# 1/rms of each token: VectorE block transpose of repeated columns in place of TensorE transposes, and a new order of work

## The chip, the cores and the metric

The kernel runs on one core of one Trainium2 chip. The metric is device time in microseconds (us), the median of several executions. The core has five engines, each with its own queue of instructions: TensorE (PE, with its weight loads shown as PEld), VectorE (DVE), ScalarE (ACT), GpSimd (POOL) and SyncE (SP), which only issues DMA transfers here.

## The reference

Two layers in a row, all in float32. First a cross read between 512 tokens and 32 state vectors for 8 batches of 8 heads with 64 features:

```python
scores = scale * np.matmul(x, state.transpose(0, 1, 3, 2))   # softmax over the 32 states
xread = np.matmul(a, state)
scores2 = scale * np.matmul(state, x.transpose(0, 1, 3, 2))  # softmax over the 512 tokens
sread = np.matmul(a2, x)
return np.concatenate([xread, sread], axis=2)
```

Then the heads are put side by side, so that each of 8 x (512 + 32) tokens has 512 features, and a gated feed-forward layer with 1536 hidden units follows:

```python
rms = np.sqrt(np.mean(x * x, axis=-1, keepdims=True) + 1e-06)
xn = x / rms * rms_g
g = xn @ w_gate
silu = g * (1.0 / (1.0 + np.exp(-g)))
val = xn @ w_val
return (silu * val @ w_out)
```

The change is about 1/rms of the 512 tokens of a batch.

## The kernel before

**Batches.** A batch's tokens never exist in full: the softmax weights aT_s (256 rows in two tiles of 128 partitions, 512 tokens along the row) are kept, and the state vectors are multiplied into w_gate and w_val for each batch (`own_weights`, L548), which gives small weights v. 1/rms is multiplied into aT_s (L434), so it is needed along the row, the same in all 128 partitions. The 256 state tokens are put through the feed-forward layer at the end (xsT, `state_norm`).

**The hidden layer.** The 1536 hidden units are worked in six pairs (0 to 5), each with gate and value. `hidden_seven` forms the 2x2 block products of a pair with seven products rather than eight. On the PE (L694) their order is: first x and first z of the pair; last x of the pair before; then the second x, the second z, y and the third x of this pair. The letters are PSUM banks: x has two, y and z one each. ScalarE copies x and z out between the products (L740, L743, L745); VectorE adds z and y into the gates g and x into c (three L756), ScalarE takes the tanh (L747), and VectorE gates with L759 and two L771 (the second reads x again); for the later pairs L775 and L781 follow. A pair's first x product needs an x bank that the second L771 of two pairs before has left, and a pair's last x product must come after its third L756, which reads x. `project_seven` does the output layer in the same manner (L856), with ScalarE copies L893 (p1, p5, u2, c21) and VectorE sums L901 and L908.

**The next batch beside it.** While batch b is in its hidden and output layers, batch b+1 has its softmax: `tokens_read` (stream "a"), `states_read` ("s"), its first two products of weights ("w"), and the copies and GpSimd sums of them ("x", L559 and L574 to L577). Steps of `tokens_read` that matter here: the transpose L289, transposes by blocks and a round through DRAM for x (L310, L313, L318), scores L328, softmax L337 to L414, the read L421, squares L428 with sums L431, then `rms_on_blocks`: a transpose by blocks L364, a sum within blocks L367, a matmul with the matrix `groups` (L370), whose result stands in PSUM as 128 partitions x 16 columns: partition 32g+t, column k holds the mean square of token 32k+t, the same in all four groups g of 32 partitions. L375, four times, takes from each group its own four columns, so that 128 partitions x 4 columns hold each token once. GpSimd raises them to the power -1/2 (L271), and the PE transposes each of the four columns, repeated 128 times, into PSUM (L278). L434 reads it there. `slot_sums` on GpSimd (L612 to L615) then forms sums of aT_s for the next batch's products.

**Order of work.** Nothing is scheduled at run time. Within the loop over batches 1 to 7, the string PERIOD gives one letter for each step: the letter's stream (a generator) is run to its next `yield`, and what it emits is queued on the engines in that order. The same string serves all seven turns; in the turn of batch 7, which has no batch after it, the letters "a" run `state_norm` and the first sums of the states' weights, one step at every third "a" (`paced`). Its steps are squares on ScalarE (L510), sums on the PE (L515), their 1e-6 on VectorE and the power on GpSimd (L519, L271), the transposes on the PE (L278), then on VectorE four L525 that scale xsT and four L679. The tiles "at" and "pv" in PSUM have two buffers each, and "xT" and "eS" in SBUF one each; every new use waits for the last reader of the one before.

Of the kernel before, what the change touches and what calls it, by code (L numbers as in the profile page):

```python
# [8 lines left out]
F32 = mybir.dt.float32  # L9
# [3 lines left out]
ALU = mybir.AluOpType  # L13
# [4 lines left out]
P = 128  # L18
# [10 lines left out]
)  # L29

PERIOD = (
    "hhvthttxhauhhxhuauaahhtutaahtahvxvtuhuxxhuuhthtxuthuhtuhhuhuhhutuhutthuxuhxtxuhh"
    "vhuuthhxthxtahuhathuuuxuuauthuthtahhuthuuuhuhpuuuhtuuucauapaaasaspkacpaspsspaaaa"
    "aaaapkkcpccaakaaascuskaappkaaaaapssssaaaaksapkakasswwwxxpxkxxpccssx"
)

STATES = (
# [6 lines left out]
def kernel(  # L44
# [21 lines left out]
    VE, SE, GE, TE = nc.vector, nc.scalar, nc.gpsimd, nc.tensor  # L66

    B, H, S, D = x.shape
    Ns = state.shape[2]
    DM = H * D  # L70
    DFF = moe_w_gate.shape[1]
    NC = S // P
# [7 lines left out]
    consts = ctx.enter_context(tc.tile_pool(name="consts", bufs=1))  # L80
    one = ctx.enter_context(tc.tile_pool(name="one", bufs=1))
    two = ctx.enter_context(tc.tile_pool(name="two", bufs=2))
# [26 lines left out]
    def load_x(b, *queues):  # L109
# [8 lines left out]
        for c in range(NC):  # L118
# [3 lines left out]

    ident = consts.tile([P, P], F32, name="ident")
    make_identity(nc, ident)
    mhalf = consts.tile([P, NC], F32, name="mhalf")
    GE.memset(mhalf, -0.5)
    ones = consts.tile([P, 1], F32, name="ones")
    GE.memset(ones, 1.0)

    GE.tensor_tensor(out=consts.tile([P, NC], F32, name="first_pow"), in1=mhalf,  # L130
                     in0=ones.to_broadcast([P, NC]), op=ALU.pow)
    bounds = consts.tile([P, 2], F32, name="bounds")
    GE.memset(bounds[:, 0:1], 1151.0 + 7.5 / 16)
# [4 lines left out]
    for i in range(4):  # L138
        GE.tensor_copy(groups[:, i], ident[:, 0:Ns])
        for j in range(1, 4):  # L140
            GE.tensor_tensor(out=groups[:, i], in0=groups[:, i],
                             in1=ident[:, Ns * j:Ns * j + Ns], op=ALU.add)
# [125 lines left out]
    def mean_root(ss, n):  # L268

        ri = two.tile([P, NC], F32, name="ri")  # L270
        GE.tensor_tensor(out=ri[:, 0:n], in0=ss, in1=mhalf[:, 0:n], op=ALU.pow)  # L271
        return ri

    def along_rows(ri, n):

        rp = aps.tile([P, NC, P], F32, name="at")
        for c in range(n):
            TE.transpose(out=rp[:, c, :], in_=ri[:, c:c + 1].to_broadcast([P, P]), identity=ident)  # L278
        return rp.rearrange("p c t -> p (c t)")
# [80 lines left out]
    def rms_on_blocks(b, sq):  # L360


        n = S // Ns
        VE.transpose(out=sq[:, 1, :], in_=sq[:, 0, :])  # L364
        yield
        part = one.tile([P, n], F32, name="part")
        VE.reduce_sum(out=part, in_=sq[:, 1, :].rearrange("p (k f) -> p k f", f=Ns), axis=AXX)  # L367
        yield
        sp = aps.tile([P, n], F32, name="at")
        TE.matmul(out=sp, lhsT=groups.rearrange("p i t -> p (i t)"), rhs=part,  # L370
                  start=True, stop=True)
        yield
        ss = two.tile([P, NC], F32, name="ss")
        for g in range(4):
            VE.tensor_scalar(ss[Ns * g:Ns * g + Ns], sp[Ns * g:Ns * g + Ns, g::4], 1e-6, None,  # L375
                             op0=ALU.add)
        yield "step"
        ri = mean_root(ss, NC)
        yield
        rp = along_rows(ri, NC)  # L380
        yield
        return rp

    def tokens_read(b):
# [45 lines left out]
        for i, j in ((0, 1), (2, 3), (0, 2)):  # L430
            VE.tensor_tensor(out=sq[:, i, :], in0=sq[:, i, :], in1=sq[:, j, :], op=ALU.add)  # L431
            yield
        rp = yield from (rms_on_array if b < 2 else rms_on_blocks)(b, sq)
        VE.tensor_tensor(out=aT_s[b], in0=aT_s[b],  # L434
                         in1=rp.unsqueeze(1).to_broadcast([P, 2, S]), op=ALU.mult)
# [71 lines left out]
    def state_norm():  # L507

        sq = one.tile([P, NI, NT], F32, name="sqT", tag="eS")
        SE.activation(out=sq, in_=xsT, func=ACTF.Square, scale=DM ** -0.5)  # L510
        yield
        sp = aps.tile([P, NT // P], F32, name="at")
        for r in range(NT // P):
            for i in range(NI):
                TE.matmul(out=sp[:, r:r + 1], lhsT=sq[:, i, P * r:P * r + P], rhs=ones,  # L515
                          start=(i == 0), stop=(i == NI - 1))
        yield
        ss = two.tile([P, NT // P], F32, name="sst")
        VE.tensor_scalar(ss, sp, 1e-6, None, op0=ALU.add)  # L519
        ri = mean_root(ss, NT // P)  # L520
        yield
        rp = along_rows(ri, NT // P)
        yield
        for i in range(NI):
            VE.scalar_tensor_tensor(out=xsT[:, i, :], in0=xsT[:, i, :], scalar=rms_g[:, i:i + 1],  # L525
                                    in1=rp[:, 0:NT], op0=ALU.mult, op1=ALU.mult)
        sums_of_x()
        yield
# [143 lines left out]
    def sums_of_x():  # L672

        tt = seven["late"].tile([P, 3, HI, P], F32, name="x_t")
        b11, b12, b21, b22 = blocks_of_x()
        x_sums.extend(tt[:, i] for i in range(3))
        for to, a, b in ((tt[:, 0], b12, b11), (tt[:, 1], b22, tt[:, 0]), (tt[:, 2], b21, tt[:, 1]),
                         (b12, b22, b12)):
            VE.tensor_tensor(out=to, in0=a, in1=b, op=ALU.subtract)  # L679
# [319 lines left out]
    for b in range(1, B):  # L999
        if b + 2 < B:  # L1000
            load_state(b + 2)
            load_x(b + 2)
        h, t, u = hidden_seven(S, weights_of(b), lambda b=b: tokens_of(b), False)
        p, c, k = project_seven(S, store_tokens(b))
        own = [own_weights(b, mp) for mp in range(2, NM // 2)]
        then = [own_weights(b + 1, mp) for mp in range(2)] if b + 1 < B else []
        others = None
        streams = {"h": h, "t": t, "u": u, "p": p, "c": c, "k": k,
                   "v": (step for part in own for step in part[0]),
                   "x": (step for part in own + then for step in part[1])}  # L1010
        if b + 1 < B:
            streams.update(a=tokens_read(b + 1), s=states_read(b + 1),
                           w=first_products(b + 1, then))
        else:
            others = paced(step for part in (state_norm(), sums_of_w([0])) for step in part)
            streams["a"] = others
        with tc.manual_schedule(**by_hand):
            for stream in PERIOD:
                if stream in streams:
                    step = next(streams[stream], done)  # L1020
                    assert step is not done or b + 1 == B
        assert all(next(stream, done) is done for stream in streams.values() if stream is not others)
    n = B * (NM // 2)
# [37 lines left out]
```

## Time and profile before

| | |
|---|---|
| time, median of 3 | 779.46 us (779.45 to 780.23) |
| span of the profiled execution | 777.7 us |
| PE busy | 765.8 us, 98% |
| DVE busy | 536.7 us, 69% |
| ACT busy | 325.6 us, 42% |
| POOL busy | 161.6 us, 21% |
| L278, transposes of 1/rms (PE) | 34, 274 ns each from start to end |
| L271, power on 128x4 (POOL) | 8, 1158 ns each |
| L375, 32x4 (DVE) | 24, 158 ns each |

The share of an engine is its busy time over the span. Matmuls overlap in the pipeline, so a mean of 274 ns is the time through it; what a matmul costs in a full stream is the distance from its start to the next one's. A line's number is that of the kernel before throughout.

### The profile page before, as it was taken

Reading aid. Unit: us, or ns where it says so; the run is one execution under the profiler, and the core shown is the slowest. Engines: PE = TensorE matmul, PEld = TensorE weight load, DVE = VectorE, ACT = ScalarE, POOL = GpSimd, SP = SyncE. Lnnn points to the kernel's source line nnn. Section 1 sums busy time; section 2 is a strip of 40 time slices with the busy share of each in tenths; the row PEclk is TensorE's granted clock in tenths of the full one; section 3 lists DMA queues with packets and bytes.
Section 4 is the critical chain, followed back from the end, with each engine's and each line's share of the span. In section 5 each row is a group of like instructions: output and inputs, shape, how many; then the busy total and the mean of one; then the engine's idle time right before and its main releaser. Section 6 shows DMA issues by size and latency. Waiting matters only on the chain.

```text
span 777.7 us, 12111 instructions
## 1 busy us (share of the span) xinstructions
PE 765.8 (98%) x4722; PEld 586.2 (75%) x4722; DVE 536.7 (69%) x846; ACT 325.6 (42%) x536; POOL 161.6 (21%) x232
## 2 busy tenths in 40 slices
PE   6999999999999999999999999999999999999998
PEld 4643344688877887878878877888778878888996
DVE  4999996678647882888468864787378735881461
ACT  4998874553135322542255314532344314510320
POOL 2100003430053104320433015400631043300000
PEclk9999999999999999999999999999999999999999
DMA  9789764670266225630466026612543154100311
GB/s 290 200 293 322 274 175 173 184 255 14 85 190 247 79 72 177 238 115 20 160 207 214 1 95 219 248 39 68 204 163 109 41 176 163 55 14 27 123 55 28
DMA packets 73689, 113.00 MB, mean 145 GB/s; under 512 B 40864, under 2 KB 51616, under 8 KB 66720
## 3 DMA queue, kind: packets, MB, share of 16 engines
q1 hardware_dynamic: 60512, 92.75, 35.1%
q10 hardware_dynamic: 13120, 19.47, 8.5%
q8 instruction: 38, 0.62, 0.3%
q14 instruction: 19, 0.16, 0.1%
HBM read 87.56 MB, written 24.64 MB: 144 GB/s over the span
## 4 chain that ended last, share of the span: by engine, by line
PE 92%; DVE 5%; DMA 1%; SPq 1%; issue 0%; ACT 0%; DVEq 0%
PE f L694 38%; PE f L856 35%; PE f L796 5%; PE pv L590 4%; PE at L548 3%; PE pv L548 3%; PE at L328 1%; DVE ex L249 1%; PE at L490 1%; PE at L421 1%; DVE raw L245 1%; DMA raw<-in_moe_w_gate_dram 1%; DVE w_m L254 1%; DVE top L242 1%; DMA rows<-in_state_dram 0%
## 5 line engine op out<-in xcount | busy, mean ns | idle before, releaser
L856 PE MATMUL f<-wo,hb 128*128 128x256 f32 x540 | 123.0, 382 | 0.0
L694 PE MATMUL f<-aT_s,v 128*128 128x256 f32 x504 | 119.7, 382 | 0.0
L856 PEld LDWEIGHTS f<-wo,hb 128*128 128x128 f32 x540 | 101.5, 190 | 23.1 <-issue 5.0
L694 PEld LDWEIGHTS f<-aT_s,v 128*128 128x128 f32 x504 | 93.6, 190 | 24.3 <-DVE c L756 5.9
L756 DVE TENSOR_TENSOR g<-g,f 128x512 f32<-128x512 f32 (+1 forms) x96 | 61.4, 651 | 68.6 <-PE f L694 40.3
L694 PE MATMUL f<-aT_t,vs 128*128 128x256 f32 x336 | 87.1, 382 | 0.0
L747 ACT ACTIVATE hb<-g 128x1024 f32<-128x1024 f32 (+1 forms) x48 | 48.2, 1004 | 87.6 <-DVE g L756 87.6
L856 PE MATMUL f<-wt,hs 128*128 128x256 f32 x360 | 80.4, 379 | 0.0
L271 POOL TENSOR_TENSOR ri<-ss,mhalf 128x4 f32<-128x4 f32 x8 | 9.3, 1158 | 340.9 <-DVE ss L375 233.5
L893 ACT COPY ot<-f 128x256 f32<-128x256 f32 x60 | 20.1, 371 | 134.7 <-PE f L856 126.0
L856 PEld LDWEIGHTS f<-wt,hs 128*128 128x128 f32 x360 | 68.3, 190 | 9.4 <-issue 0.2
L694 PEld LDWEIGHTS f<-aT_t,vs 128*128 128x128 f32 x336 | 63.2, 190 | 14.9 <-issue 5.9
L759 DVE SCALAR_TENSOR_TENSOR hb<-hb,g 128x1024 f32<-128x1024 f32 x42 | 53.8, 1282 | 13.1 <-ACT hb L747 13.1
L574 POOL TENSOR_TENSOR vs<-v 128x256 f32<-128x256 f32 x42 | 30.5, 726 | 144.2 <-ACT v L559 144.2
L559 ACT COPY v<-pv 128x512 f32<-128x512 f32 x42 | 22.9, 595 | 67.7 <-PE pv L548 67.7
L745 ACT COPY g<-f 128x512 f32<-128x512 f32 (+1 forms) x48 | 26.9, 559 | 56.3 <-PE f L694 56.3
L796 PE MATMUL f<-wo,hb 128*128 128x512 f32 x96 | 44.7, 600 | 0.0
L590 PE MATMUL pv<-aT_s,v 128*128 128x512 f32 x96 | 43.7, 595 | 0.2 <-DVE aT_s L434 0.2
L694 PE MATMUL f<-aT_s,vs 128*128 128x256 f32 x168 | 43.1, 379 | 0.0
L694 PE MATMUL f<-aT_t,v 128*128 128x256 f32 x168 | 43.1, 379 | 0.0
L856 PE MATMUL f<-wo,hs 128*128 128x256 f32 x180 | 41.5, 382 | 0.0
L856 PE MATMUL f<-wt,hb 128*128 128x256 f32 x180 | 40.8, 383 | 0.0
(142 smaller groups left out, 1241.1 us busy)
## 6 DMA issues: line engine op xcount, KB each, us to landing
w_m<-w_d SPq DMA_DIRECT2D x48, 1024.0 KB, 5.7
out_dram<-ot SPq DMA_DIRECT2D x56, 128.0 KB, 1.8
raw<-in_moe_w_val_dram SPq DMA_DIRECT2D x6, 1024.0 KB, 5.5
raw<-in_moe_w_out_dram SPq DMA_DIRECT2D x6, 1024.0 KB, 7.8
x_b<-in_x_dram SPq DMA_DIRECT2D x96, 64.0 KB, 2.4
w_d<-w_m SPq DMA_DIRECT2D x6, 1024.0 KB, 4.9
x_d<-xB ACTq DMA_DIRECT2D x6, 1024.0 KB, 4.3
xG<-x_d ACTq DMA_DIRECT2D x24, 256.0 KB, 5.0
```

Of the source, the lines that this page charges most:

```text
L548: TE.matmul(out=pv[e][Ns * j:Ns * j + Ns, :], lhsT=stT_g[b][D * e:D * e + D, j, :], rhs=w[D * e:D * e + D, j].rearrange("p m k f -> p (m k ...
L559: SE.copy(v[:, e].rearrange("p m k f -> p (m k f)"), pv[e])
L574: GE.tensor_tensor(out=vs[:, 0], in0=a21, in1=a22, op=ALU.add)
L590: TE.matmul(out=to[0], lhsT=lhs(i, k), rhs=r, start=(i == 0), stop=(i == len(rhs) - 1))
L694: TE.matmul(out=ps[:, i, 0:half], lhsT=l[:, i, :], rhs=r, start=(start and i == 0 and k == 0), stop=(k == len(lhs) - 1), skip_group_check= ...
L745: SE.copy(gates(q)[1], q["x"][:, :, 0:half])
L747: SE.activation(out=hb[:, 2 * mp:2 * mp + 2, 0:n].rearrange("p m (c t) -> p m c t", c=2), in_=q["g"][:, :, :, 0:half], func=ACTF.Silu if s ...
L756: VE.tensor_tensor(out=to, in0=to, in1=q[ps][:, :, 0:half], op=ALU.add)
L759: VE.scalar_tensor_tensor(out=h, in0=h, scalar=1.0, op0=ALU.add, op1=ALU.mult, in1=q["g"].rearrange("p m c t -> p m (c t)"))
L796: TE.matmul(out=banks[r], lhsT=hb[:, m, P * r:P * r + P], rhs=wo[:, m, :], start=(m == 0), stop=(m == NM - 1))
L856: TE.matmul(out=banks[name][:, r, :], lhsT=lhs(k)[:, P * r:P * r + P], rhs=rhs(k), start=(start and r == 0 and k == 0), stop=(k == HM - 1) ...
L893: SE.copy(to, banks[name][:, r, :])
```

## The change

In batches 2 to 7 each group of 32 partitions keeps all 16 columns, so it holds 1/rms of all 512 tokens. A VectorE transpose works on blocks of 32x32, within a group of 32 partitions: given column k repeated 32 times, it puts token 32k+t at place t of block k in every one of the 32 partitions. So one instruction lays 1/rms along the row in all 128 partitions, and the four PE transposes and their PSUM tile are not needed; the result goes into a free part of sq in SBUF. Batches 0 and 1 (`rms_on_array`) and the states keep the PE's way. PERIOD is dealt anew for this, with as many steps of each stream as before, and `state_norm` loses two of its `yield`s.

```diff
-    mhalf = consts.tile([P, NC], F32, name="mhalf")
+    mhalf = consts.tile([P, S // Ns], F32, name="mhalf")
...
 def rms_on_blocks(b, sq):
...
-        ss = two.tile([P, NC], F32, name="ss")
-        for g in range(4):
-            VE.tensor_scalar(ss[Ns * g:Ns * g + Ns], sp[Ns * g:Ns * g + Ns, g::4], 1e-6, None,
-                             op0=ALU.add)
+        ss = two.tile([P, n], F32, name="ssb")
+        VE.tensor_scalar(ss, sp, 1e-6, None, op0=ALU.add)
         yield "step"
-        ri = mean_root(ss, NC)
-        yield
-        rp = along_rows(ri, NC)
+        ri = two.tile([P, n], F32, name="rib")
+        GE.tensor_tensor(out=ri, in0=ss, in1=mhalf, op=ALU.pow)
+        yield
+        rp = sq[:, 2, :]
+        VE.transpose(out=rp, in_=ri.unsqueeze(2).to_broadcast([P, n, Ns]))
         yield
         return rp
...
 def state_norm():
...
                 TE.matmul(out=sp[:, r:r + 1], lhsT=sq[:, i, P * r:P * r + P], rhs=ones,
                           start=(i == 0), stop=(i == NI - 1))
-        yield
         ss = two.tile([P, NT // P], F32, name="sst")
         VE.tensor_scalar(ss, sp, 1e-6, None, op0=ALU.add)
         ri = mean_root(ss, NT // P)
         yield
         rp = along_rows(ri, NT // P)
-        yield
         for i in range(NI):
             VE.scalar_tensor_tensor(out=xsT[:, i, :], in0=xsT[:, i, :], scalar=rms_g[:, i:i + 1],
                                     in1=rp[:, 0:NT], op0=ALU.mult, op1=ALU.mult)
```

The new PERIOD moves, on the PE, the scores L328 from the output layer into the last pairs of the hidden layer, the read L421 from behind the second wt,hs group of L856 to ahead of it, the first two L548 of the next batch to straight behind L370, L490 into the middle of the last L856 group, and the L548 of pairs 3 and 4 forward within pair 0 of the hidden layer. On VectorE the blocks' transposes and the softmax move with them. PERIOD itself:

```diff
-    "hhvthttxhauhhxhuauaahhtutaahtahvxvtuhuxxhuuhthtxuthuhtuhhuhuhhutuhutthuxuhxtxuhh"
-    "vhuuthhxthxtahuhathuuuxuuauthuthtahhuthuuuhuhpuuuhtuuucauapaaasaspkacpaspsspaaaa"
-    "aaaapkkcpccaakaaascuskaappkaaaaapssssaaaaksapkakasswwwxxpxkxxpccssx"
+    "hhvthtaxhxthauhvuvthhtauhthxhaahtuuxxuxahuhuatthtuuhxhhuutuxhuhthhuhuttauhxthhhu"
+    "ahuuuavhattuhtxuhhxhutuuauuthaaauhaxhhthtutuhuhuhuuuaptuuuhupuacpaaaaaaaapaaaapa"
+    "kacaakapssaaaaaspcsspakcakkcaaucksaawwsxwxppxksssxppskkpsxskpcxsscs"
```

More of the change, by code (lines that the diff above doesn't have):

```diff
@@ L128 @@
     GE.memset(ones, 1.0)
-    GE.tensor_tensor(out=consts.tile([P, NC], F32, name="first_pow"), in1=mhalf,
+    GE.tensor_tensor(out=consts.tile([P, NC], F32, name="first_pow"), in1=mhalf[:, 0:NC],
                      in0=ones.to_broadcast([P, NC]), op=ALU.pow)
```

## The prediction

> **What bounds the kernel now.** I read the page's busy shares first, then the list of waits of the PE, the PE's timeline over one whole batch, and last the timelines of the batch where the state norm runs.
>
> The busy shares and the chain of work that ended last:
>
> ```profile
> PE 765.8 (98%) x4722; PEld 586.2 (75%) x4722; DVE 536.7 (69%) x846; ACT 325.6 (42%) x536; POOL 161.6 (21%) x232
> PE 92%; DVE 5%; DMA 1%; SPq 1%; issue 0%; ACT 0%; DVEq 0%
> ```
>
> The PE is never free and the chain runs through it. A busy PE is not proof by itself, so the list of what PE matmuls waited for comes next:
>
> ```profile
> PE at L289 <- DMA rows<-in_state_dram: 5.9, 1, 5.9
> PE at L548 <- DVE w_m L254: 0.9, 1, 0.9
> PE at L328 <- ACT xT L302: 0.7, 1, 0.7
> PE at L348 <- DVE sq L431: 0.6, 1, 0.6
> PE pv L590 <- DVE aT_s L434: 0.2, 1, 0.2
> ```
>
> All of these lie in the opening stage. In batches 1 to 7 the PE waits for nothing, so in them time is won only by taking work off the PE, and lost by any wait that reaches it. The PE's timeline round the edited steps of one period:
>
> ```profile
> 374.47 2.75 PE L856 MATMUL f<-wo,hs 128*128 128x256 f32 x12
> 377.06 0.29 PE L370 MATMUL at<-part,groups 128*128 128x16 f32 x2
> 377.20 2.84 PE L856 MATMUL f<-wo,hs 128*128 128x256 f32 x12
> 379.88 0.60 PE L278 MATMUL at<-ident,ri 128*128 128x128 f32 x4
> 380.41 1.10 PE L490 MATMUL at<-x_b,e2T 128*32 128x64 f32 x64
> 381.44 1.09 PE L548 MATMUL pv<-w_m,stT_g 64*32 64x512 f32 x16
> ```
>
> Columns are start, length, what. Read starts against starts: the four transposes hold the PE from 379.88 to 380.41, 0.53 us. One period is 83.47 us (the score matmuls of L328 start at 181.92 and at 265.39 in the chain).
>
> [...] L364 and L310 transpose 128x512 in blocks in 0.69 to 0.71 us. [...] VectorE sits 4.45 us before L756 in each period, held by a wait that the view puts on L289. [...]
>
> **The change part by part.**
>
> *Batches 2 to 7, PE.* Four transposes go, six times. The slot is 0.53 us; ahead of it 0.09 us is lost (the L856 group begun at 377.20 has 12 passes of 0.2158, 2.59, and the next thing starts 2.68 later). So at most 0.62 a period. But the new order on the PE sets L490 alone between two L856 groups. Where it stands alone in the opening stage it holds the PE 1.12 us instead of 1.03 and leaves 0.08 on either side: 0.25 us given back. Between 0.27 and 0.62, I take 0.4: 6 x 0.4 = 2.4 us saved (1.6 to 3.7). All other PE work is the same instructions in another order.
>
> *Batches 2 to 7, VectorE and GpSimd.* Four L375 of 0.16 us become one of about 0.2; a transpose of 128x512 (0.7 by L364) is added. The power goes from 4 columns (1.16 us by L271) to 16. Two columns took 0.70, so 0.23 a column and an estimate of 3.9 us; the other bound is 1.2. Behind it on VectorE wait the transpose, L434 and the L901 of p5; behind it on GpSimd the slot sums. In the new order L370 comes 18.9 us ahead of the next batch's first product (two L548 groups, 60 passes of L856, L490, L502), where it was 11.6. With sum 0.5, power 3.9, transpose 0.7, L434 1.2 and four slot sums of 0.73 the chain needs about 9.5 us: hidden, at either bound. The L901 on p5 has to be done before the wt,hb products; that is 12.3 us after L370, and it needs about 8.
>
> *The other moves in a period.* Score matmuls move ahead of the last products of pair 4; from them to L421 the PE now has 20.8 us of work, and VectorE needs it for two pairs of gates and the softmax. Counting its starts in the trace (0.60 a 512-column pass, 1.2 for L759, 2.65 from L407 to L414), the second aT_s half is done about 1.5 us ahead of L421. The L548 pair at mp 0 and 1, moved up behind L370, needs a PSUM buffer that L374 frees: 0.6 us ahead. For xG the last load is issued about 7.7 us ahead and lands in 5.0 (6.3 at most). I cost these at nothing; the hiding work is the PE's own queue.
>
> *Batch 7, state norm.* This is the part I charge. Two yields went, so the sum L519 and the power are issued in one step with the matmuls L515, and L525 and the four L679 in one step with L278. Before, they were steps apart:
>
> ```profile
> 646.40 1.84 PE L515 MATMUL at<-ones,sqT 128*128 128x1 f32 x16
> 648.28 0.16 DVE L519 TENSOR_SCALAR sst<-at 128x2 f32<-128x2 f32 x1
> 674.78 0.38 PE L278 MATMUL at<-ident,ri 128*128 128x128 f32 x2
> 685.91 1.65 DVE L525 SCALAR_TENSOR_TENSOR xsT<-xsT,rms_g,at 128x256 f32<-128x256 f32 x4
> 687.48 0.42 DVE L679 TENSOR_TENSOR x_t<-xsT 128x256 f32<-128x256 f32 x1
> ```
>
> L519 met a result just ready, and L525 ran 10.7 us after L278, in the projection, where nothing on the PE stood behind it. In the changed kernel's order VectorE has L519 straight behind the third add (L756, c) of pair 0, and ahead of pair 0's L759 and L771. The PE has L515 only after the second z product of pair 1. Take 0 as the start of batch 7's first product (639.14 before), 0.864 us a product:
> - The PE comes to L515 at 12.8. Its PSUM tile is one of the two of the L548 pair; ScalarE empties that behind pair 1's L745, at about 13.2. L515 runs 13.3 to 15.0: 0.5 us of wait.
> - VectorE, idle since 7.3, does L519 at 15.2, L759, L771, L771 until 17.8 (1.26 + 0.61 + 0.68). The last frees the x bank that pair 2's first product needs. The PE is there at 16.7 and starts at about 18.1: 1.3 us.
> - L278 follows at 19.0 to 19.2, L525 and L679 from 19.5 (3.16 us by the starts 685.91 and 689.07), and only then the L756 add of pair 1, done at 23.4. Pair 1's last product must not write x before it; it would have run at 20.1: 3.4 us.
>
> Queued behind these waits on VectorE are pair 0's and pair 1's gates, and the PE waits for both. Sum 5.2 us, in one batch, once. After it VectorE is again ahead of the PE, and the work moved forward (L651 and L653 into pairs 3 to 5) leaves c of pairs 4 and 5 0.6 to 0.8 us to spare. The projection gets nothing in return, since the PE had no wait there.
>
> *Sum.* 779.46 - 2.4 + 5.2 = 782.3 us.
>
> **The rivals.**
> 1. The wait in batch 7 is absorbed and only the PE's saving remains: 779.46 - 2.4 = 777.1, faster. For it: six batches have the clean gain. Against: the x bank and the add of pair 1 are true dependences, and VectorE is in order. 0.16.
> 2. Half of the wait shows, because the L515 result comes earlier than I place it or VectorE does L525 and L679 quicker: 2.4 us against 2.4, 779.5, the same. Against: 1.57 and 1.59 us for these eight are measured. 0.08.
> 3. On top of the forecast a wait appears in each period, at L421 or at L328 where I have 1.5 us to spare: some 0.7 x 6 = 4, so 786.3. For it: softmax and gates now share VectorE. Against: margins by the trace's own durations. 0.10.
> 4. The forecast, 0.66.
>
> **How the numbers follow.** With saving 1.6 to 3.7 and wait 4.3 to 6.0 (without the L515 part, or with 0.3 more on each wait), the forecast covers 780.1 to 783.9. Rival 1 reaches down to 777.0 with the estimate of 2.4 us. The upper end, 785.5, leaves most of rival 3 outside. Range 777.0 to 785.5. Of the forecast's 0.66 about 0.04 lies within 0.2% (below 781.0), so slower 0.62 + 0.10 = 0.72, same 0.04 + 0.08 = 0.12, faster 0.16.
>
> **What would show it.** Right: no L278 in batches 2 to 7, the L328 to L328 period at about 83.1, no PE wait in it; in batch 7 the PE waits on VectorE's L771 and on the c add of L756, the stretch from batch 7's first product to its first L856 grows from 41.9 us to about 47, and VectorE shows a long wait for L515. Wrong: batch 7's stretch unchanged, or a period above 83.5 (then L421, L328 or L374 is where I look), or a power far above 5 us.

## The result, and the profile after

The changed kernel takes 789.47 us (median of four, 788.03 to 791.89) against 779.46 us before: a ratio of 1.0132, 95% interval 1.0104 to 1.016, some 10 us slower. The profiled execution is at the lower end, 788.03 us, with a span of 786.2 us against 777.7: 8.5 us to account for in the traces. From L517 of the kernel before on, the changed kernel's numbers are one or two lower (L519 is now L518, L525 is L523, L548 is L546, L694 is L692, L756 is L754, L771 is L769, L856 is L854); the lines above keep theirs, but the new transpose is L380.

The busy shares and the chain that ended last, of the changed kernel:

```profile
PE 764.7 (97%) x4698; PEld 583.2 (74%) x4698; DVE 540.6 (69%) x834; ACT 325.0 (41%) x536; POOL 179.6 (23%) x232
PE 82%; DMA 8%; DVE 8%; issue 1%; ACTq 1%; ACT 0%; SPq 0%
```

The 24 transposes are gone (4722 to 4698 PE instructions) and 1.1 us of PE busy time with them, but the chain no longer runs through the PE alone: DMA has gone from 1% of it to 8%, VectorE from 5% to 8%. What the PE waited for (us in total, times, longest), the five lines of the list that are new:

```profile
PE at L490 <- DMA e2T<-e_d: 5.2, 5, 2.0
PE f L692 <- DVE c L754: 3.1, 1, 3.1
PE f L692 <- DVE hb L769: 1.0, 1, 1.0
PE at L515 <- ACT v L557: 0.3, 1, 0.3
PE at L490 <- issue: 0.2, 1, 0.2
```

The waits for c, hb and v are the state norm in batch 7. The two at L490, 5.4 us in six times, are in the periods. The PE's timeline in the first of them (start, length, what, and in brackets the idle time before and what ended it):

```profile
201.96 0.29 PE L370 MATMUL at<-part,groups 128*128 128x16 f32 x2
202.18 1.09 PE L546 MATMUL pv<-w_m,stT_g 64*32 64x512 f32 x16
203.06 1.06 PE L546 MATMUL at<-w_m,stT_g 64*32 64x512 f32 x16
...
218.41 1.10 PE L490 MATMUL at<-x_b,e2T 128*32 128x64 f32 x64 [1.13 <-DMA e2T<-e_d]
```

L490 needs the exponents of the states' read, which go from eB to DRAM (e_d, L475) and come back transposed (e2T, L479). The chain of waits in the same stretch:

```profile
203.95 1.17 DVE eB L472
...
205.14 8.78 DMA e_d<-eB
...
215.34 2.98 DMA e2T<-e_d
```

The write takes 8.78 us. Over the six batches, from the view of line L475, in the changed kernel:

```profile
DMA to landing us min/median/max: 7.6/7.8/9.1
```

Before, the same view of the same line:

```profile
DMA to landing us min/median/max: 2.6/2.6/3.6
```

What lies in front of the write is seen in the timeline of the two issuing queues (SPq is SyncE's, ACTq ScalarE's):

```profile
203.40 1.19 SPq L169 DMA_DIRECT2D w_m<-w_d  x2
...
205.14 0.35 ACTq L475 DMA_DIRECT2D e_d<-eB  x1
```

The two L546 at 202.18 and 203.06 are the last readers of two weight buffers, so as they finish, SyncE fetches the next two weights, 1024 KB each. In the kernel before these L548 stood behind L490, which had started at 380.41, and the loads went out after it:

```profile
368.31 0.35 ACTq L475 DMA_DIRECT2D e_d<-eB  x1
...
382.90 1.53 SPq L169 DMA_DIRECT2D w_m<-w_d  x2
```

The write itself does not go out later than before: it is issued 12.1 us ahead of L490 there (368.31 and 380.41), and 12.1 us ahead of the time at which the PE comes to L490 here (205.14 and 217.28).

The periods, from the first L328 of a batch to that of the next, are 84.34, 85.21, 83.40, 84.10 and 83.93 us, where each was 83.47 to 83.48. The idle times before L490 in them are 1.13, 2.01, 0.19, 0.89 and 0.72, and 0.44 in batch 7's preparation: 5.4 us together. Each period is 83.2 and its idle time.

In batch 7, the timelines of the PE and VectorE:

```profile
655.79 1.95 PE L515 MATMUL at<-ones,sqT 128*128 128x1 f32 x16 [0.30 <-ACT v L557]
657.77 0.16 DVE L518 TENSOR_SCALAR sst<-at 128x2 f32<-128x2 f32 x1 [7.95 <-PE at L515]
660.53 1.10 PE L692 MATMUL f<-aT_s,v 128*128 128x256 f32 x4 [0.97 <-DVE hb L769]
661.89 1.66 DVE L523 SCALAR_TENSOR_TENSOR xsT<-xsT,rms_g,at 128x256 f32<-128x256 f32 x4 [0.31 <-PE at L278]
665.05 0.68 DVE L754 TENSOR_TENSOR c<-c,f 128x512 f32<-128x512 f32 x1
665.79 1.13 PE L692 MATMUL f<-aT_t,v 128*128 128x256 f32 x4 [3.07 <-DVE c L754]
```

VectorE stands 7.95 us at L518 with the gates of pair 0 behind it, and the PE waits for them (hb). Behind L278, L523 and four L677 stand ahead of pair 1's last addition (c), and the PE waits again. The hidden layer from the first product (642.53) to the first L854 (689.63) is 47.1 us, where it was 41.9 (the three brackets of the PE are 4.3 of these 5.2; a wait can hide in the modelled ends of the matmuls ahead of it); from there to the end nothing comes back (96.6 us in both).

So the 8.5 us of the two traces are 5.2 in batch 7, 5.4 before L490, and about 2.0 won back. Of these 2.0 some 0.4 us lie in the opening (batch 1's first product at 134.78, before at 135.16), whose length varies by as much from trace to trace. The rest of the 10 us between the medians is in executions other than the profiled one.

### The profile page after: what moved, and what is told of

Its sections match the earlier page's. It is cut to its first block, busy times and chain, and to the rows that moved or that the text cites. A ratio compares the mean times of both kernels' runs of the same rounds, so it can differ in the third digit from the quotient of the medians.

```text
span 786.2 us, 12078 instructions
## 1 busy us (share of the span) xinstructions
PE 764.7 (97%) x4698; PEld 583.2 (74%) x4698; DVE 540.6 (69%) x834; ACT 325.0 (41%) x536; POOL 179.6 (23%) x232
## 4 chain that ended last, share of the span: by engine, by line
PE 82%; DMA 8%; DVE 8%; issue 1%; ACTq 1%; ACT 0%; SPq 0%
PE f L692 37%; PE f L854 27%; DMA e_d<-eB 5%; PE f L794 5%; PE pv L588 4%; PE at L546 3%; DMA e2T<-e_d 2%; PE pv L546 2%; PE at L328 1%; DVE ex L249 1%; PE at L490 1%; PE at L421 1%; DVE raw L245 1%; ACTq L479 1%; DVE eB L472 1%
## 5 line engine op out<-in xcount | busy, mean ns | idle before, releaser
L854 PE MATMUL f<-wo,hb 128*128 128x256 f32 x540 | 123.9, 382 | 0.0
L692 PE MATMUL f<-aT_s,v 128*128 128x256 f32 x504 | 120.7, 382 | 1.0 <-DVE hb L769 1.0
L854 PEld LDWEIGHTS f<-wo,hb 128*128 128x128 f32 x540 | 101.5, 190 | 23.1 <-issue 9.9
L692 PEld LDWEIGHTS f<-aT_s,v 128*128 128x128 f32 x504 | 94.0, 190 | 24.7 <-issue 12.4
L692 PE MATMUL f<-aT_t,vs 128*128 128x256 f32 x336 | 87.8, 384 | 0.0
L754 DVE TENSOR_TENSOR g<-g,f 128x512 f32<-128x512 f32 (+1 forms) x96 | 61.3, 651 | 33.9 <-PE f L692 26.1
L854 PE MATMUL f<-wt,hs 128*128 128x256 f32 x360 | 80.4, 379 | 0.0
L692 PEld LDWEIGHTS f<-aT_t,vs 128*128 128x128 f32 x336 | 62.6, 190 | 20.4 <-issue 11.7
L572 POOL TENSOR_TENSOR vs<-v 128x256 f32<-128x256 f32 x42 | 32.8, 780 | 188.2 <-ACT v L557 188.2
L854 PEld LDWEIGHTS f<-wt,hs 128*128 128x128 f32 x360 | 68.3, 190 | 9.4 <-issue 0.2
L377 POOL TENSOR_TENSOR rib<-ssb,mhalf 128x16 f32<-128x16 f32 x6 | 19.7, 3289 | 177.2 <-DVE ssb L374 177.2
L899 DVE TENSOR_TENSOR ot<-ot,f 128x256 f32<-128x256 f32 x45 | 17.4, 414 | 58.7 <-PE f L854 54.3
L557 ACT COPY v<-at 128x512 f32<-128x512 f32 x54 | 29.1, 593 | 56.0 <-POOL vs L575 31.1
L692 PE MATMUL f<-aT_t,v 128*128 128x256 f32 x168 | 43.3, 380 | 3.1 <-DVE c L754 3.1
L692 PE MATMUL f<-aT_s,vs 128*128 128x256 f32 x168 | 43.1, 379 | 0.0
L854 PE MATMUL f<-wt,hb 128*128 128x256 f32 x180 | 41.8, 383 | 0.0
```

What stands on the lines that cost most here:

```text
L557: SE.copy(v[:, e].rearrange("p m k f -> p (m k f)"), pv[e])
L572: GE.tensor_tensor(out=vs[:, 0], in0=a21, in1=a22, op=ALU.add)
L692: TE.matmul(out=ps[:, i, 0:half], lhsT=l[:, i, :], rhs=r, start=(start and i == 0 and k == 0), stop=(k == len(lhs) - 1), skip_group_check= ...
L754: VE.tensor_tensor(out=to, in0=to, in1=q[ps][:, :, 0:half], op=ALU.add)
L854: TE.matmul(out=banks[name][:, r, :], lhsT=lhs(k)[:, P * r:P * r + P], rhs=rhs(k), start=(start and r == 0 and k == 0), stop=(k == HM - 1) ...
```

## The experiments

The theory after the first reading, T: the loss is the order's, in two parts that have nothing to do with each other, the wait of the state norm in batch 7 and the write of e_d behind two weight loads; the 1/rms code itself saves. Rival 1: the longer chain of 1/rms (the power on GpSimd, the transpose on VectorE) holds the periods up. Rival 2: the PE's new order costs time on the PE itself.

**rms_alone.** The new 1/rms code in the kernel before; PERIOD and the two yields stay.

```diff
...
-        ri = mean_root(ss, NC)
-        yield
-        rp = along_rows(ri, NC)
+        ri = two.tile([P, n], F32, name="rib")
+        GE.tensor_tensor(out=ri, in0=ss, in1=mhalf, op=ALU.pow)
+        yield
+        rp = sq[:, 2, :]
+        VE.transpose(out=rp, in_=ri.unsqueeze(2).to_broadcast([P, n, Ns]))
```

> The new 1/rms code (one add, pow of 128x16, one block transpose) in the order of the kernel before, with both yields of the state norm kept. Theory (the loss comes from the order: state norm in batch 7, and the e_d write queued with the w_m loads): no L490 wait, e_d lands in under 4 us, stretch of batch 7 near 41.8 us, and what is left is the clean saving of a period without L278: between 0.07 us (the one waitless period of after, 83.40 against 83.47) and the 0.4 us of the prediction, times 6: 777.0 to 779.1 us. Rival 1 (the longer pow and the longer chain on VectorE hold up each period): first products of batches 2 to 7 come later, periods of 83.8 or more, 781 us or more.

Measured: 785.27 us, ratio 1.0069 (1.0055 to 1.0082). The expectation of T missed; the time is that of rival 1. The write lands in 2.6 us and there is no L490 wait, but every period is 84.45 to 84.46. VectorE and the PE in one of them (L380 is the new transpose, L498 the read of L490's PSUM tile, L548 the next user of that tile):

```profile
382.52 0.71 DVE L380 STREAM_TRANSPOSE sq<-rib 128x512 f32<-128x512 f32 x1 [2.11 <-POOL rib L377]
...
384.59 0.47 DVE L498 TENSOR_SCALAR sr<-at,z 128x64 f32<-128x64 f32 x2
385.20 1.09 PE L548 MATMUL at<-w_m,stT_g 64*32 64x512 f32 x14 [0.37 <-DVE sr L498]
```

L498 could have run when L490 had ended, at about 382.9. In VectorE's order it stands behind L380 and L434, and L380 waits for the power. Through L498 that reaches the PE: from L490 to the L856 behind the L548 pair it is 4.33 us, where it was 2.90 (the bracket has 0.37 of the 1.43; the rest is counted as busy time of the two L548 matmuls ahead, whose ends are modelled). So the chain does cost time in the old order, though not as its own length, and the next run asks whether this is all.

**sr_first.** rms_alone with a few letters of PERIOD moved, so that L498 comes ahead of L380.

```diff
-    "aaaapkkcpccaakaaascuskaappkaaaaapssssaaaaksapkakasswwwxxpxkxxpccssx"
+    "aaaapkkcpccaakaaascuskaappkaaaaapssssaaaaksapkkssaawwwxxpxkxxpccssx"
```

> The kernel rms_alone (new 1/rms code in the order of before) with three letters of PERIOD moved, so that VectorE does L498 (the read of the PSUM tile that L548 waits for) ahead of the transpose L380, which waits for the pow. Theory (what rms_alone lost, 1.0 us a period, is L498 held up in VectorE's own order behind the pow of 2.9 to 3.3 us, and the saving of L278 itself is real): L548 no longer waits, periods of 83.05 to 83.2 us against 83.47, that is 2.0 to 2.5 us under before: 776.5 to 777.5 us. Rival (the pow or the block transpose slows the period in another way): periods stay at 84.4, 785 us.

Measured: 776.79 us, ratio 0.9961 (0.9948 to 0.9973), under the kernel before. Every period is 83.04. The same place (the power takes 2.91 us in both runs):

```profile
379.24 0.48 DVE L498 TENSOR_SCALAR sr<-at,z 128x64 f32<-128x64 f32 x2 [0.64 <-PE at L490]
379.63 0.70 DVE L380 STREAM_TRANSPOSE sq<-rib 128x512 f32<-128x512 f32 x1
379.99 1.06 PE L548 MATMUL at<-w_m,stT_g 64*32 64x512 f32 x16
```

L380 no longer waits, since the power has ended by the time L498 is done, and L548 no longer waits either. No wait of the PE is left in the periods, and this is the saving in the old order: 0.43 us a period, 2.6 in six.

**order_alone.** The changed kernel with the old `rms_on_blocks`: the diff of the 1/rms code undone, PERIOD and the yields as changed.

```diff
-        ss = two.tile([P, n], F32, name="ssb")
-        VE.tensor_scalar(ss, sp, 1e-6, None, op0=ALU.add)
+        ss = two.tile([P, NC], F32, name="ss")
+        for g in range(4):
+            VE.tensor_scalar(ss[Ns * g:Ns * g + Ns], sp[Ns * g:Ns * g + Ns, g::4], 1e-6, None,
+                             op0=ALU.add)
...
-        GE.tensor_tensor(out=ri, in0=ss, in1=mhalf, op=ALU.pow)
-        yield
-        rp = sq[:, 2, :]
-        VE.transpose(out=rp, in_=ri.unsqueeze(2).to_broadcast([P, n, Ns]))
+        ri = mean_root(ss, NC)
+        yield
+        rp = along_rows(ri, NC)
```

> The new order and the yields taken out, with the old 1/rms code (four adds, pow of 128x4, along_rows with its matmuls L278). Theory: the whole loss of after stays, and L278 comes back on top, 0.1 to 0.4 us a period: 790 to 792 us, e_d landing in 7 us or more, L490 wait of about 1 us a period, stretch of batch 7 near 47. Rival 1 (the new 1/rms code costs the time in the periods): periods fall back to about 83.5 and only batch 7's 5.2 us stay: 784 to 786 us.

Measured: 811.41 us, ratio 1.0405 (1.039 to 1.0421); both forecasts missed by 19 us or more. In its list of PE waits:

```profile
PE at L278 <- POOL ri L271: 14.2, 6, 2.4
```

In the new order L278 comes on the PE straight behind L370, before add and power can be done. 2.4 us of a period of 87.1 to 88.2 is this wait. The PE's timeline behind it:

```profile
204.83 0.65 PE L278 MATMUL at<-ident,ri 128*128 128x128 f32 x4 [2.43 <-POOL ri L271]
205.41 1.09 PE L546 MATMUL pv<-w_m,stT_g 64*32 64x512 f32 x16
206.29 2.02 PE L546 MATMUL at<-w_m,stT_g 64*32 64x512 f32 x16
```

The second L546 takes 2.02 us where it takes 1.06 in the changed kernel: fourteen of its matmuls start only when L434 on VectorE, which reads L278's result in PSUM, has ended (it runs from 205.95 to 207.17). These 0.96 us, the wait of 2.43 and 0.58 for L278 itself make 87.2 of 83.2. Two of the five periods are that long (87.11 and 87.18); in the other three slower passes come on top (in the third the second L546 takes 2.84 us, and the L854 group behind it 5.69 where 5.45 is usual), and the mean granted clock of the execution is 0.987. The write of e_d lands in 3.0 us (2.6 to 4.1) here: the L546 pair is held up behind L278, and the weight loads with it (206.62 in the same period, behind the write at 205.95). As a test of T the run says little. It shows that the order needs the new code; rms_alone shows that the code needs another order than the old one.

**fetch_behind.** The changed kernel with one thing moved: the two weight loads that the early L546 release go out on ScalarE's queue behind the fourth e2T load.

```diff
-    def fetch(n):
+    held = []
+
+    def fetch(n, queue=nc.sync):
         if NM // 2 <= n < (B + 1) * (NM // 2):
-            nc.sync.dma_start(out=new_w(n), in_=w_d[n % (NM // 2)])
+            queue.dma_start(out=new_w(n), in_=w_d[n % (NM // 2)])
...
                                     in_=e_d[b % 2][:, :, g].rearrange("j t f -> t j f"))
+                while g == 3 and held:
+                    fetch(held.pop(0), nc.scalar)
                 yield
...
-            fetch(b * (NM // 2) + mp + W_BUFS)
+            if b > 1 and mp < 2:
+                held.append(b * (NM // 2) + mp + W_BUFS)
+            else:
+                fetch(b * (NM // 2) + mp + W_BUFS)
```

> After, with the two w_m loads of mp 0 and 1 held back and issued on ScalarE's queue behind the fourth e2T load, instead of right behind the L546 that free their buffers. Theory: the e_d write lands in 2.6 to 4 us again, PE no longer waits at L490, the periods come to 83.1 to 83.5 us, and 3.5 to 5.2 us go: 784.3 to 786.0 us, with batch 7's norm wait (stretch of 47) unchanged. Rival 1 (pow and VectorE chain) and rival 2 (a slower order of matmuls on PE itself): periods stay at 84 us, 788.5 to 790 us.

Measured: 783.14 us, ratio to before 1.005 (1.0033 to 1.0067), 6.3 us under the changed kernel's 789.47 and 1.2 under the range that T gave. The write and L490 (L476 and L493 here):

```profile
DMA to landing us min/median/max: 2.6/2.6/4.3
```

```profile
383.94 1.10 PE L493 MATMUL at<-x_b,e2T 128*32 128x64 f32 x64
```

No wait, and all five periods are 83.14. Rival 1 and rival 2 fall for the new order: with the same chain of 1/rms and the same order on the PE the periods are 0.33 shorter than before.

**one_behind.** As fetch_behind, but only one of the two loads is put behind.

```diff
-            if b > 1 and mp < 2:
+            if b > 1 and mp == 1:
```

> As fetch_behind, but only one of the two w_m loads (mp 1) is put behind the e2T loads; the one of mp 0, 1024 KB, stays in front of the e_d write. Theory (time to landing grows with the bytes queued ahead, and PE waits only once it passes about 7.4 us, the shortest landings of after having given waits of 0.2 us): e_d lands in 4 to 6 us, no wait at L490, 782.5 to 784 us, as with both behind. Rival (each load costs its share of the loss): half of it stays, about 785.5 to 786.5 us.

Measured: 783.78 us, ratio 1.0053 (1.0038 to 1.0069). The write (L476):

```profile
DMA to landing us min/median/max: 4.6/5.4/6.6
```

Nothing ahead, one load, two loads: 2.6, 5.4, 7.8 us at the median. The time is fetch_behind's. The PE waits at L493 once, 0.4 us, and there it was not the write (5.2 us) that was long, but a load of e2T behind it, with 5.58 us where 3 are usual. The longest write, 6.6 us, made nothing wait, and in the changed kernel one of 7.8 us cost 0.19: the order leaves the write 4 to 5 us of room, and the loss begins where that is used up.

**pow_twice.** fetch_behind with each power done twice.

```diff
-        GE.tensor_tensor(out=ri, in0=ss, in1=mhalf, op=ALU.pow)
+        for _ in range(2):
+            GE.tensor_tensor(out=ri, in0=ss, in1=mhalf, op=ALU.pow)
```

> fetch_behind with the pow of each period done twice on GpSimd, 3.3 us more ahead of the transpose in six periods. Theory (in the new order pow and transpose have about 10 us to spare before the first matmul that takes the slot sums): no change, 782.7 to 783.8 us. Rival (the chain of 1/rms is on the path in the new order as in rms_alone): 1 to 3 us more per period, 789 us or more.

Measured: 783.09 us, ratio 1.005 (1.0033 to 1.0066), periods 83.14, though GpSimd's pair takes 6.27 us. In fetch_behind's order the power is hidden with room to spare.

**norm_late.** The changed kernel with the state norm of batch 7 begun later.

```diff
+LATE = 18
...
-    def paced(steps):
+    def paced(steps, late):
+        yield from range(late)
         while True:
...
-            others = paced(step for part in (state_norm(), sums_of_w([0])) for step in part)
+            others = paced((step for part in (state_norm(), sums_of_w([0])) for step in part), LATE)
```

> After, with 18 of the letters a of batch 7 let go by before the state norm starts, so that its matmuls L515 and L278 and its VectorE work come about where the kernel before had them (behind the last pairs of the hidden layer). Theory: the stretch of batch 7's hidden layer falls from 47.1 to 41.8-42.3 us, the waits of L692 on c and hb go, 5.2 us less: 783.8 to 785.0 us, periods and L490 waits unchanged. Rival: the norm was hidden in after too, or its wait is only moved to the states' first products: 788 us or more.

Measured: 785.82 us, ratio 1.0087 (1.0056 to 1.0117), six executions from 781.23 to 789.92; the median is 0.8 us above the range that was expected. The waits on c and hb are gone. From batch 7's first product to the end of the profiled span it is 139.6 us (143.7 in the changed kernel, 138.6 before): 4.1 of the 5.2 are won. L515 and L278 came too late this time, both in the projection, and the PE waits for the power there:

```profile
699.91 0.43 PE L279 MATMUL at<-ident,ri 128*128 128x128 f32 x2 [1.04 <-POOL ri L272]
```

The L490 waits are all still there, 7.4 us in the profiled execution, which is the slowest of the six; that the spread comes from them is not shown, since the other five have no trace.

**both.** fetch_behind, with the two yields back and the norm's steps set by hand at letters a of batch 7, so that L515 comes 15.4 us and L278 35.7 us after the first product, and the VectorE work behind the last pair.

```diff
+        yield
         ss = two.tile([P, NT // P], F32, name="sst")
...
         rp = along_rows(ri, NT // P)
+        yield
         for i in range(NI):
...
-            if next(steps, done) is done:
-                break
-            yield from range(3)
+        for k in itertools.count():
+            if k in (0, 6, 9, 13, 17) or k > 17 and k % 4 == 0:
+                if next(steps, done) is done:
+                    break
+            yield
```

> After with both causes taken out: the two w_m loads of mp 0 and 1 issued behind the e2T loads, and the state norm of batch 7 with its two yields back and its five steps at the letters a number 0, 6, 9, 13 and 17, so that L515 comes behind pair 2, the pow behind pair 4's sums, L278 in pair 6 and the VectorE work behind the last pair. Theory: the losses add (5.2 us in batch 7, 4.9 us at L490), periods of 83.14, stretch of batch 7 near 41.8: 783.1 - 5.2 = 777.9 us, range 777.3 to 778.5, 1 to 2 us under before. Rival (the two waits partly hide each other): 780 us or more.

Measured: 777.40 us, ratio 0.9972 (0.9962 to 0.9982), faster than before. The PE waits for nothing from batch 7's first product to its projection, and from that product to the end it is 138.6 us, as before. The two losses add: 6.3 us from the loads, 5.7 from the norm, and what remains against before is the saving of six periods. The profiled execution, 779.26 us, is the slowest of the eight, and the others are at most 777.72. In it one period is 84.66 instead of 83.14: there the four loads of xG landed in 7.9 to 9.3 us (4.9 at the median in the changed kernel), and the PE waited for them at the scores, L330 here. In the other traces no such wait shows.

## Why the prediction was wrong

The forecast was 782.3 us, in a range from 777.0 to 785.5; measured were 789.47. The direction held, and so did the charge it rested on. One term, put at nothing, was 5.4 us in the profile.

- *What bounds the kernel*: right. Whatever was followed up here moved the time by PE work removed, by a wait that reached the PE, or, in norm_late, by slower passes behind such a wait (granted clock 0.66 over five us).
- *The saving, 2.4 us*: the mechanism holds and the size is a little high for this order. It is 0.33 us a period, 2.0 in six, by fetch_behind, and 0.43 a period by sr_first, in the old order. The difference of 0.10 is all that the new order costs on the PE, L490 standing alone included, and 0.25 had been set aside for that; the slot itself gave less than the 0.62 it was taken from.
- *Batch 7, state norm, 5.2 us*: right in sum and in its places. VectorE kept the order it was given, as the forecast took it to: it stood 7.95 us at L518, with the gates of pair 0 behind it. L515 began 13.26 us after the first product (13.3 said), L518 at 15.24 (15.2), the x product of pair 2 at 18.0 (18.1), the last x product of pair 1 at 23.26 (23.4). The waits themselves show as 0.30, 0.97 and 3.07 us against 0.5, 1.3 and 3.4. The stretch is 47.1 us, and both takes 5.7 off by undoing it.
- *The power*: 3.29 us against an estimate of 3.9, hidden, as said; pow_twice shows it would be at double the length. The estimate started from 1.16 us for 128x4, a mean over eight that the opening's power of 1.99 us raises; in the periods it took 1.02. From there and the 0.70 of two columns it is 0.16 a column and 2.9 us, which is what rms_alone shows.
- *The other moves in a period*, costed at nothing: this step failed. L421, L328 and L374 were looked at, and none of them waits in the changed kernel. Of the moved L548 pair the prediction asked what it needs, a PSUM buffer, and not what it gives free. Its end releases two weight loads of 1024 KB, and 15 us ahead of L490 they go in front of the 512 KB write that L490 depends on. The prediction names neither the loads nor the write, so the write's landing of 2.6 us, true of the old order, stood for the new one too; it was 7.8. The missing term is 5.4 us in the profile, and 6.3 between the medians of after and fetch_behind. With it the sum is 779.46 - 2.0 + 5.2 + 5.4 = 788.1, where the profiled execution was 788.03; that it comes so close is partly luck, since the median is 1.4 us above that and 0.4 of the 2.0 lay in the opening.
- *The rivals*: the third, a further wait in each period at 786.3 us, had the right form, a wait in each period, and the wrong place. The first two, less loss in batch 7, did not occur. The range's upper end, 785.5, took in batch 7's wait and little of a second one.

The prediction did not ask why the L548 pair had been moved. rms_alone and sr_first show what the old order does with the new code: a read of a PSUM tile that the PE wants back stands behind VectorE's wait for the power. Moving the pair is one way out of that, and it brought the wait for the write; moving L498 is another, and no wait of the PE came of it.

What stays open: how much of the changed kernel's 1.5 us between its profiled execution and the difference of the medians is the clock, below, and why xG landed late in one execution of the run both.

## What to carry to other kernels

When work is moved forward, list what its end releases, not only what it waits for: here two buffers that came free started two loads, and a write that had landed in 2.6 us without them landed in 7.8 behind them. A landing time read in the old order is a property of that order; before a transfer is costed at it again, look up what will be in flight beside it, and how much room its reader has. (The 1024 KB write of x_d, too, lands in 7.9 us at the median in the changed kernel, 4.3 before; no wait came of it.) And an instruction that waits on a slower engine should be dealt behind any read that gives a PSUM tile back to the PE: with L380 ahead of L498 the periods were 84.45 us, behind it 83.04.

## What the runs showed of the hardware

A write on one queue landed later with large loads issued ahead of it on another: 512 KB on ScalarE's queue landed in 2.6, 5.4 and 7.8 us at the median with none, one and two loads of 1024 KB issued ahead of it on SyncE's (fetch_behind, one_behind and the changed kernel). Each load ahead added 2.4 to 2.8 us, about as much as the whole write takes alone.

The power's time on GpSimd grew with the columns in these runs, and was not the same in every order of work. Beside the same VectorE instructions it took 1.02 us for 128x4 (before) and 2.92 for 128x16 (rms_alone), about 0.16 a column; in the new order 1.52 for 128x4 (order_alone) and 3.29 for 128x16. Batch 7's power of 128x2 took 0.70 us before and 1.62 in the changed kernel. What makes these differ was not tested. The VectorE block transpose of 128x512 took 0.71 us at L364, and at L380 too, where its input is 16 columns, each read 32 times.

A wait of the PE cost more than its length in two places of norm_late. After its longest wait at L490 (L491 there), the timeline and the busy time of the stretch behind (its last columns are the granted PE clock, the DMA share and GB/s):

```profile
304.37 1.10 PE L491 MATMUL at<-x_b,e2T 128*32 128x64 f32 x64 [2.45 <-DMA e2T<-e_d]
305.40 4.54 PE L855 MATMUL f<-wt,hb 128*128 128x256 f32 x12
```

```profile
305.00:310.00 5.00, 5.00 (x49) 4.04 (x38) 0.48 (x2) 0.02 (x1) 0.00 (x0) 0.66 0.14 30
```

Twelve passes that take 2.86 us in other periods take 4.54: 1.7 us on top of the 2.45. The granted clock was 0.66 in these five us, and 1.00 in the five before and the five behind. It came again after a wait of 2.01 us in the same execution: the twelve passes took 3.97 us, with a granted clock of 0.83 from 640 to 650. After the waits of 0.77 and 0.73 us in it the passes took 2.86. The changed kernel's wait of 2.01 us had no such end: the passes behind it took 2.86, with a granted clock of 1.00 from 304 to 308. So the length of the wait alone does not settle it, and what does was not tested.

The changed kernel's execution with the longest span, 790.1 us, is also that with the lowest mean granted clock, 0.994, where the other three have 0.998. How much of its spread the clock makes was not shown.
